# Soft-capped attention followed by soft mixture-of-experts on one core: other parts and packets for the second-layer weights, other places for the weight loads, and shorter dispatch sums

## The chip, the cores and the metric

The kernel runs on 1 core of one Trainium2 chip, as one launch. The time is device microseconds (us) of that core. Before the change three runs gave 284.57 us in the median (280.42, 284.57 and 288.0). The core has five engines with their own instruction streams: TensorE (PE: matmuls, weight loads, transposes), VectorE (DVE), ScalarE (ACT), GpSimd (POOL) and SyncE (SP). DMA transfers run on 16 DMA engines, and reach them here by two queues: SP's (q1, plain copies) and POOL's (q0, which also casts float32 to bfloat16 on the way; called the casting queue below).

## The reference

Attention with 8 batches, 12 heads, 448 tokens and 64 dimensions a head, float32:

```python
scores = q @ k.T / 8;  scores = 30 * tanh(scores / 30)
attn = softmax(scores);  x = attn @ v            # -> x: 3584 tokens x 768
```

Then a soft mixture of experts with 8 experts of 4 slots each (32 slots), w1 of 8 x 768 x 1024 and w2 of 8 x 1024 x 768:

```python
logits = x @ phi                                  # 3584 x 32
d = softmax(logits, over all 3584 tokens)         # dispatch
slot_in = d.T @ x                                 # 32 x 768
slot_out[e] = relu(slot_in[e] @ w1[e]) @ w2[e]    # 4 slots for each expert
c = softmax(logits, over the 32 slots)            # combine
out = c @ slot_out                                # 3584 x 768
```

No output can be written before the dispatch sums over all tokens are complete, both layers of the experts have run, and so all of w1 and w2 have been read.

## The kernel before

**Attention.** Work goes by quads of four heads (24 quads, Q) and by pairs of heads (48 pairs). A quad's q and k come in by casting DMAs (`load`, two 224-KB loads a quad, started when the transposes of the quad two earlier have freed the buffer), are turned by PE (`K`, `J`) and copied by DVE (`k`, `j`). Scores of three 128 x 448 chunks lie in one PSUM tile (`Q`, L432); ACT takes tanh from it (`T`, L442); six chunks form a group, whose exp is done either by ACT (`E`, L446) or by eight DVE steps that build it as a polynomial (`p`, L466 to L474). PE multiplies by v (`A`, `B`, `t`, `u`, L495), DVE normalises (`r`, `m`), PE turns x (`X`, `y`), and a batch's logits (`L`), their exp (`e`), dispatch sums (`S`, added up by `s`) and transposed exps (`R`, `c`) follow.

**The order** is written out by hand as a string of jobs, `PROGRAM`, for all engines at once; every engine runs its part of it in that order. Three kinds of job are only fillers for PE: `N` (a 128x512 matmul into a spare tile), `F` (57 columns) and `G` (64 columns).

**Weights.** `M` jobs start a casting DMA of weights each, on POOL, in the order of `wjobs`: 16 halves of w1 (768 KB each in bfloat16), which stay in SBUF; then the parts of w2 that SBUF has no room for, which are cast into DRAM tiles (`w2d`, "spilled" or parked); then three kept parts of w2 (`w2u`) that go to SBUF. There are 64 blocks of w2, each of 128 rows; a part is four blocks. A part holds the same 128 rows of four experts, so a packet of it is one row of 768 elements (1536 bytes written). 6 parts are parked whole; 7 are parked as two halves of 384 columns (768 bytes a packet).

**Reload.** When attention tiles come free, SP copies the parked parts back to SBUF (`reload`, L162): 20 loads, 6 of 768 KB and 14 of 384 KB. One (job `O0`) goes out in `PROGRAM`, the others behind it, each waiting for the tiles whose place it takes. The order of SP's queue is: v loads, these 20, then the output.

**The end.** Layer 1 (L859), relu, transposes of the hidden values (`h_transp`, L876), then layer 2 (`layer2`, L887) in two sweeps over the 16 parts: first the left 384 columns of all (half 0), then the right 384 (half 1). The accumulated half goes to SBUF as `so[0]` (L935) and `so[1]` (L943). Eight left half-tiles of output are computed between the parts of the second sweep (`EARLY`, L916 to L920) and stored at once (L904); the rest of the 28 token tiles follow, DVE and ACT in turn, with the stores on SP.

**Dispatch sums.** `slot_sums` gives, for a batch, the 193 columns of slot inputs and of the sum of exps z; `z_mms` (L599) makes z with 16 matmuls of one column, four for each group of tokens so that it stands in all four groups of 32 partitions. `slot_add` (L664) adds them up in `slz`, and `zacc`, its last column, is inverted into `rz` at the end.

Of the kernel before, what the change touches and what calls it, by code (L numbers as in the profile page):

```python
# [9 lines left out]
F32 = mybir.dt.float32  # L10
BF16 = mybir.dt.bfloat16
# [27 lines left out]
def kernel(  # L39
# [31 lines left out]
    WHOLE = 6  # L71
# [28 lines left out]
    slz = consts.tile([P, NJ * NS + 1], F32, name="slacc")  # L100
    slacc = slz[:, 0:NJ * NS].rearrange("p (j s) -> p j s", s=NS)
    zacc = slz[:, NJ * NS:]
# [12 lines left out]
    blocks = [(i, ft, gg) for i in range(E // 4) for ft in range(NFT) for gg in range(4)]  # L115

    def w2_src(n0, n):

        i, ft, gg = blocks[n0]
        return bass.AP(tensor=moe_w2.tensor,  # L120
                       offset=((4 * i + gg) * F + ft * P) * D,
                       ap=[[D, P], [F * D, n], [1, D]])
# [8 lines left out]
    def load_part(dst, n0, half=None):  # L131
        src = w2_src(n0, 4)
        if half is not None:
            src = bass.AP(tensor=src.tensor, offset=src.offset + half * HD,
                          ap=[[D, P], [F * D, 4], [1, HD]])
        pool.dma_start(out=dst, in_=src)
# [3 lines left out]
    late = len(w2_parts) - KEPT + NFREE  # L140
    w2_kept = w2_parts[:NFREE] + w2_parts[late:]
    w2_spilled = [(n0, None) for n0 in w2_parts[NFREE:NFREE + WHOLE]]
    w2_spilled += [(n0, half) for half in range(2) for n0 in w2_parts[NFREE + WHOLE:late]]

    dram = ctx.enter_context(tc.tile_pool(name="dram", bufs=1, space=bass.MemoryType.DRAM))
    w2d = {(n0, half): dram.tile([P, 4, D if half is None else HD], BF16, name=f"w2d{n0}_{half}")
           for n0, half in w2_spilled}
    wjobs += [(load_part, w2d[part], *part) for part in w2_spilled]
# [12 lines left out]
    def reload(n, t):  # L161
        sp.dma_start(out=t, in_=w2d[w2_spilled[n]])  # L162
        w2t[w2_spilled[n]] = t

    def reload_raw(n):
        t = rawt[:, 2 - 2 * n:4 - 2 * n, :].rearrange("p n s -> p (n s)")
        reload(WHOLE + n, t[:, 0:4 * HD].rearrange("p (n d) -> p n d", d=HD))

# [29 lines left out]
p0.4 M0 T5 Q6 k2 p0.5 N1.0 T6.1 Q7 N3.0 V1.0 j2 V1.1 T7 Q8 p0.6 T8.6 Q9 N3.0 p3.0 T9 Q10 M1 p3.1  # L198
N1.0 T10.3 Q11 p0.7 J3.0 E2 p3.2 A0.1 t0 j3 B0 u0 p3.3 K3.0 Q12 T11 G14.12 k3 G6.12 p3.4 T12.4 Q13
r0 p3.5 A1.0 M2 T13 Q14 t1 B1 m0 T14.2 F8 u1 Q15 r1 m1 T15 p3.6 N1.0 X0.0 y0 J4.1 E4 x0 p7.0 A2.0  # L200
Q16 p3.7 t2 M3 F9 E5 j4 B2 u2 p7.1 K4.1 k4 Q17 p7.2 T16.7 A3.1 r2 p7.3 B3 t3 u3 T17 Q18 G6.18 m2
T18.0 r3 p7.4 N1.0 A4.0 Q19 M4 m3 E6 F12 p7.5 J5.1 t4 F4 B4 j5 T19 p7.6 Q20 K5.1 T20.5 Q21 k5 u4 r4
A5.1 T21 p7.7 t5 B5 m4 M5 E8 u5 p10.0 X1.0 Q22 r5 p10.1 y1 Q23 x1 G19.23 T22.6 p10.2 N1.0 K6.0 m5
T23 Q24 p10.3 X2.1 T24.3 y2 Q25 x2 M6 k6 T25 Q26 p10.4 J6.0 T26.1 L0.1 j6 p10.5 Q27 e0 E11 S0.1
p12.0 A6.0 p10.6 B6 Q28 E9 t6 u6 G23.28 r6 s0 M7 m6 R0.1 p12.1 A7.0 T27 c0 B7 p12.2 t7 u7 K7.1 T28.2
r7 k7 m7 E13 p12.3 A8.0 J7.1 Q29 p10.7 Q30 F9 M8 p12.4 T29 B8 G13.30 j7 T30.4 p12.5 Q31 t8 J8.1 T31
u8 Q32 r8 p12.6 T32.7 Q33 G6.33 m8 T33 Q34 p15.0 K8.0 j8 M9 T34.0 p15.1 N1.1 A9.1 t9 E14 p12.7 B9
p15.2 u9 Q35 k8 N1.0 Q36 p15.3 T35 A10.0 t10 B10 T36.5 r9 p15.4 u10 Q37 m9 M10 T37 Q38 p15.5 J9.1
T38.6 Q39 j9 G6.39 r10 T39 p15.6 A11.1 t11 B11 E16 u11 Q40 r11 m10 G10.40 m11 K9.0 p18.0 A12.1 t12
# [623 lines left out]
    for n in (0, WHOLE + 2, WHOLE + 3, 1, 2, 3, WHOLE + 1, *range(4, WHOLE), *range(WHOLE + 4, len(w2_spilled))):  # L833
        if n == WHOLE + 1:
            reload_raw(1)
            continue
# [7 lines left out]
    def w2_half(n, half):  # L844
        n0 = n - n % 4
        if (n0, half) in w2t:
            return w2t[n0, half][:, n % 4, :]
# [164 lines left out]
```

## Time and profile before

| | |
|---|---|
| median of 3 runs | 284.57 us (280.42 to 288.0) |
| the profiled execution's own time | 281.34 us |
| its span, first to last instruction | 279.4 us |
| granted TensorE clock, mean | 0.968 |
| ACT busy | 245.1 us, 88% |
| DVE busy | 242.2 us, 87% |
| PE busy | 236.1 us, 85% |
| casting queue (q0) | 31840 packets, 35.77 MB, 75.1% of 16 DMA engines' span |
| SP's queue (q1) | 22880 packets, 32.95 MB, 35.8% |

The attention fills the time to about 235 us; experts and output fill the rest. The share of a queue is the time that its packets took over 16 engines' time; packets of the two queues may be under way in one engine together, so the sum can pass 100%. A group's row gives line, engine, operation, tiles and count, then busy time and the mean of one in ns, then the idle time of the engine ahead of it and who ended it. In the page's rows by slices of the span one slice is a fortieth.

### The profile page before, as it was taken

The numbers are of one execution on the slowest core, as the hardware profiler recorded it, in microseconds if no ns is written. First come the engines' busy times: TensorE is split into PE (matmuls) and PEld (weight loads), VectorE is DVE, ScalarE is ACT, GpSimd is POOL, SyncE is SP. The second block draws the span as 40 slices with busy tenths as digits, with TensorE's granted clock in tenths as the row PEclk, the third lists the DMA queues.
The fourth block names the chain that finished last, engine by engine and source line by source line (L and its number), as shares of the span: only waits on it lengthen the run. The fifth ranks groups of instructions, "written<-read, shape, count | busy, mean of one in ns | idle before, by whom it ended". The sixth has DMA issues, their size and how long they took to land.

```text
span 279.4 us, 9803 instructions
## 1 busy us (share of the span) xinstructions
PE 236.1 (85%) x4151; PEld 150.8 (54%) x4151; DVE 242.2 (87%) x361; ACT 245.1 (88%) x192; POOL 157.6 (56%) x253
## 2 busy tenths in 40 slices
PE   8899889987998988988888898988898998997710
PEld 6435555653565656565665665656566686543300
DVE  3799999998999999999999999999999995337740
ACT  4999999998899999999999999999999997246620
POOL 8489777365586578466885678989725420200000
PEclk9999999997799999999999999999999999999975
DMA  6999999999999999999999999999999999979996
GB/s 181 214 170 220 223 222 223 225 216 223 218 225 229 225 211 227 228 227 218 219 227 228 208 221 219 218 213 216 227 223 245 286 296 405 406 284 378 422 424 268
DMA packets 55051, 69.56 MB, mean 249 GB/s; under 512 B 5984, under 2 KB 45024, under 8 KB 55008
## 3 DMA queue, kind: packets, MB, share of 16 engines
q0 software_dynamic: 31840, 35.77, 75.1%
q1 hardware_dynamic: 22880, 32.95, 35.8%
q8 instruction: 32, 0.52, 0.7%
q10 hardware_dynamic: 288, 0.23, 0.3%
q14 instruction: 11, 0.09, 0.1%
HBM read 93.68 MB, written 21.23 MB: 411 GB/s over the span
## 4 chain that ended last, share of the span: by engine, by line
ACT 44%; DVE 21%; PE 16%; DMA 9%; issue 3%; POOL 2%; DVEq 0%; POOLq 0%; ACTq 0%
ACT ex L442 21%; ACT ex L446 11%; DMA raws<-in_q_dram 6%; ACT exg L442 6%; ACT exg L446 4%; PE pv L495 4%; DVE xq L507 3%; PE sc L432 3%; PE so_ps L887 2%; DMA out_dram<-ob 2%; DVE ex L473 2%; PE hp L859 2%; DVE xf L468 2%; DVE xp L470 2%; DVE xp L472 2%
## 5 line engine op out<-in xcount | busy, mean ns | idle before, releaser
L442 ACT ACTIVATE ex<-sc 128x1344 f16<-128x1344 f32 (+1 forms) x87 | 108.8, 1365 | 2.2 <-PE sc L432 2.1
L432 PE MATMUL sc<-qT,kT 64*128 64x448 bf16 x384 | 68.1, 357 | 8.5 <-ACT ex L442 5.2
L446 ACT ACTIVATE ex<-ex 128x2688 bf16<-128x2688 f16 x27 | 68.4, 2553 | 0.0
L495 PE MATMUL pv<-vbd,ex 128*128 128x65 bf16 (+2 forms) x1041 | 55.5, 201 | 5.4 <-DVE xT L564 1.9
L407 POOL CAST vbd<-vraw 128x384 bf16<-128x384 f32 x46 | 34.1, 742 | 42.4 <-DMA vraw<-in_v_dram 16.5
L495 PEld LDWEIGHTS <-ex 128*128 128x128 bf16 (+1 forms) x1070 | 42.9, 101 | 20.5 <-issue 5.7
L411 POOL CAST vbd<-vraw 64x64 bf16<-64x64 f32 x92 | 48.0, 521 | 2.8
L442 ACT ACTIVATE exg<-sc 128x1344 f16<-128x1344 f32 x26 | 33.2, 1344 | 1.0 <-PE sc L432 1.0
L432 PEld LDWEIGHTS <-kT 64*128 64x128 bf16 x384 | 19.1, 94 | 24.5 <-issue 11.1
L507 DVE TENSOR_TENSOR xq<-pv,rec 128x448 bf16<-128x448 f32 x47 | 28.5, 613 | 0.4
L446 ACT ACTIVATE exg<-exg 128x2688 bf16<-128x2688 f16 x11 | 27.6, 2510 | 0.0
L389 PEld LDWEIGHTS <-raws 128*64 128x64 bf16 x616 | 19.9, 111 | 12.4 <-issue 10.4
L472 DVE TENSOR_TENSOR xp<-xp,xf 128x2688 f16<-128x2688 f16 x17 | 26.4, 1555 | 0.0
L470 DVE TENSOR_TENSOR xp<-xp,xf 128x2688 f16<-128x2688 f16 x17 | 26.2, 1544 | 0.0
L278 POOL DMA_DIRECT2D raws<-in_q_dram x22 | 18.2, 827 | 13.7 <-PE qps L389 8.4
L473 DVE TENSOR_TENSOR ex<-ex,xp 128x2688 uint16<-128x2688 uint16 x15 | 23.1, 1541 | 0.0
L495 PE MATMUL pv<-vbd,exg 128*128 128x65 bf16 (+2 forms) x322 | 20.9, 201 | 2.5 <-DVE xq L507 1.3
L278 POOL DMA_DIRECT2D raws<-in_k_dram x22 | 16.9, 770 | 8.6 <-PE kps L389 8.5
L495 PEld LDWEIGHTS <-exg 128*128 128x128 bf16 (+1 forms) x322 | 14.6, 102 | 8.1 <-issue 4.1
L389 PE MATMUL kps<-ident,raws 128*64 128x128 bf16 x308 | 13.1, 225 | 3.0 <-DVE qT L401 0.9
L471 DVE TENSOR_SCALAR xp<-xp 128x2688 f16<-128x2688 f16 x17 | 15.6, 918 | 0.0
L469 DVE TENSOR_SCALAR xp<-xf 128x2688 f16<-128x2688 uint16 x17 | 14.9, 874 | 0.0
(134 smaller groups left out, 379.0 us busy)
## 6 DMA issues: line engine op xcount, KB each, us to landing
w1b<-in_moe_w_dram POOLq DMA_DIRECT2D x16, 768.0 KB, 12.7
out_dram<-ob SPq DMA_DIRECT2D x8, 768.0 KB, 7.5
vraw<-in_v_dram SPq DMA_DIRECT2D x92, 64.0 KB, 5.7
w2d<-in_moe_w_dram POOLq DMA_DIRECT2D x14, 384.0 KB, 12.0
raws<-in_q_dram POOLq DMA_DIRECT2D x22, 224.0 KB, 10.5
raws<-in_k_dram POOLq DMA_DIRECT2D x22, 224.0 KB, 11.1
w2d_None<-in_moe_w_dram POOLq DMA_DIRECT2D x6, 768.0 KB, 14.5
w2t<-w2d_None SPq DMA_DIRECT2D x6, 768.0 KB, 9.1
```

The lines of the kernel that those rows point to most:

```text
L278: pool.dma_start(out=t, in_=quad_ap(nm, Q))
L389: pe.transpose(dst, src[:, h, c * DH:(c + 1) * DH], ident)
L407: pool.tensor_copy(part(t[:, h, :, :], 0, [(CS + 2) * W, 2], [W, CS], [1, DH]), part(raw, 0, [(CS + 1) * DH, 2], [DH, CS], [1, DH]))
L411: pool.tensor_copy(t[r, h, CS + n, 0:DH], raw[r, CS * DH:(CS + 1) * DH])
L432: pe.matmul(sc[:, u, 0:S], qkT["k", Q][r, at:at + P], qkT["q", Q][r, :, n * HP:n * HP + HP], start=(c > 0 or n == 0), stop=(c > 0 or n == 1))
L442: act.activation(exs[j][:, half * CS + u0:half * CS + u1, :].bitcast(F16), sc[:, u0:u1, 0:S], ACT.Tanh, scale=qk_scale / cap)
L446: act.activation(exs[j][:, u0:u1, :], exs[j][:, u0:u1, :].bitcast(F16), ACT.Exp, scale=cap)
L470: lambda: dve.tensor_tensor(p, p, f, op=ALU.mult),
L472: lambda: dve.tensor_tensor(p, p, f, op=ALU.mult),
L473: lambda: dve.tensor_tensor(y, y, p, op=ALU.add),
L495: pe.matmul(out_, exs[j][:, u, q0:q0 + (HP if tail else P)], v_, start=(c == 0 and g == gs[0] < NF), stop=(c >= NT - 2), skip_group_check= ...
L507: dve.tensor_tensor(xq[Q][:, h, s0:s1, :], pv[:, 0:s1 - s0, 0:DH], recs.pop(pr).to_broadcast([P, s1 - s0, DH]), op=ALU.mult)
```

## The change

- **Parts and packets of w2.** A block is still 128 rows of one expert, but a part is now four blocks (512 rows) of the same expert, two parts to an expert. Within a pair of blocks the rows are dealt in turn (even rows to one, odd to the other), so a partition reads two rows that stand side by side and a packet holds 3072 bytes. `h_transp` takes the hidden values in the same order, by every second element.
- **Kept and parked.** Parts 0 to 2 are kept, parts 3 to 15 are parked whole, in 13 casting DMAs instead of 20. Each weight matmul still takes 4 blocks side by side; the four column groups now hold four blocks of the same expert and sum up in the last product.
- **Reload.** 16 loads in place of 20: parts 3 and 4 in two loads of two blocks each (384 KB), parts 5 to 14 whole (768 KB), part 15 as two column halves (384 KB, 768 bytes a packet). Left and right halves of a part otherwise come together.
- **Places of `M`.** 32 jobs instead of 39, set at other places in `PROGRAM`; 5 of the `N` jobs and two `F4` are gone, one `G23` is `G25`, one `G12` is `G11`; all other jobs stand in the same order.
- **Dispatch sums.** z of a batch by 4 matmuls of 32 columns instead of 16 of one; `slot_add` adds 224 columns instead of 193; two DVE operations pick the sum out by the identity once, at the end.

```diff
-    WHOLE = 6
+    WHOLE = 10
...
-    blocks = [(i, ft, gg) for i in range(E // 4) for ft in range(NFT) for gg in range(4)]
+    blocks = [(e, ft) for e in range(E) for ft in range(NFT)]
...
-                       offset=((4 * i + gg) * F + ft * P) * D,
-                       ap=[[D, P], [F * D, n], [1, D]])
+        return bass.AP(tensor=moe_w2.tensor, offset=(e * F + ft * P) * D,
+                       ap=[[2 * D, P], [2 * P * D, 2], [1, 2 * D]])
...
+    w2_kept = w2_parts[:KEPT]
+    split = len(w2_parts) - WHOLE - 1
+    w2_spilled = w2_parts[KEPT:]
...
+    reload_tl(split)
+    reload_tl(split - 2, 2, 4)
+    reload_tl(split - 1, 0, 2)
+    for n in range(split + 1, split + 4):
+        reload_tl(n)
+    reload_raw(1)
+    for n in range(split + 4, split + WHOLE):
+        reload_tl(n)
+    for half in range(2):
+        reload_tl(split + WHOLE, 0, 4, half, half + 1)
...
-        z_mms(b, ps[:, SW:SW + 1], True, True)
-        slot_mms(b, ps[:, 0:SW].rearrange("p (j s) -> p j s", s=NS), range(NG), range(NJ))
+        slot_mms(b, sums, range(NF), range(NJ))
+        for g in range(NF):
+            pe.matmul(twice(ps[:, SW:SW + NS], SW + NS), ones, twice(es[b][:, g, :], 0), start=False, stop=False,
+                      skip_group_check=True)
+        pe.matmul(ps[:, SW:SW + NS], ones[0:HP, :], es[b][0:HP, NF, :], start=False, stop=True,
+                  skip_group_check=True)
+        slot_mms(b, sums, (NF,), range(NJ))
...
+    dve.tensor_tensor(zps, ident.rearrange("p (a s) -> p a s", s=NS),
+                      bass.AP(tensor=zsum.tensor, offset=zsum.offset, ap=[zsum.ap[0], [0, 4], [1, NS]]),
+                      op=ALU.mult)
+    dve.reduce_sum(zacc, zps.rearrange("p a s -> p (a s)"), axis=mybir.AxisListType.X)
...
-            pe.matmul(src[:, ft - t0, :, :], hbs[i][:, ft * P:(ft + 1) * P], own,
+            pe.matmul(src[:, ft - t0, :, :], hbs[i].rearrange("p (q f r) -> p q f r", r=2, f=P)[:, ft // 2, :, ft % 2], own,
```

The first lines of `PROGRAM` before and after (a letter is a kind of job, the numbers its arguments):

```diff
-p0.4 M0 T5 Q6 k2 p0.5 N1.0 T6.1 Q7 N3.0 V1.0 j2 V1.1 T7 Q8 p0.6 T8.6 Q9 N3.0 p3.0 T9 Q10 M1 p3.1
+p0.4 T5 Q6 k2 p0.5 N1.0 T6.1 Q7 N3.0 V1.0 j2 V1.1 T7 Q8 M0 p0.6 T8.6 Q9 N3.0 p3.0 T9 Q10 p3.1 N1.0
...
-A5.1 T21 p7.7 t5 B5 m4 M5 E8 u5 p10.0 X1.0 Q22 r5 p10.1 y1 Q23 x1 G19.23 T22.6 p10.2 N1.0 K6.0 m5
-T23 Q24 p10.3 X2.1 T24.3 y2 Q25 x2 M6 k6 T25 Q26 p10.4 J6.0 T26.1 L0.1 j6 p10.5 Q27 e0 E11 S0.1
+m4 E8 u5 p10.0 X1.0 Q22 M4 r5 p10.1 y1 Q23 x1 G19.23 T22.6 p10.2 K6.0 m5 T23 Q24 p10.3 X2.1 T24.3 y2
+Q25 x2 k6 T25 Q26 p10.4 J6.0 T26.1 L0.1 j6 p10.5 Q27 e0 E11 S0.1 M5 p12.0 A6.0 p10.6 B6 Q28 M6 E9 t6
```

More of the change, by code (lines that the diff above doesn't have):

```diff
@@ L885, in layer2 @@
         for n in range(n0, n0 + 4):
-            i, ft, gg = blocks[n]
-            pe.matmul(so_ps[half][32 * gg:32 * gg + NS, :],
-                      hpad[:, 4 * i + gg, ft, :],
+            e, ft = blocks[n]
+            pe.matmul(so_ps[half][32 * (n - n0):32 * (n - n0) + NS, :],
+                      hpad[:, e, ft, :],
                       w2_half(n, half),
```

148 lines of the change are left out of this document (70 added, 78 removed).

## The prediction

> **What bounds the kernel now.** First the page: how busy each engine and each queue is, and when.
>
> ```profile
> PE 236.1 (85%) x4151; PEld 150.8 (54%) x4151; DVE 242.2 (87%) x361; ACT 245.1 (88%) x192; POOL 157.6 (56%) x253
> ACT  4999999998899999999999999999999997246620
> DMA  6999999999999999999999999999999999979996
> q0 software_dynamic: 31840, 35.77, 75.1%
> L442 ACT ACTIVATE ex<-sc 128x1344 f16<-128x1344 f32 (+1 forms) x87 | 108.8, 1365 | 2.2 <-PE sc L432 2.1
> L442 ACT ACTIVATE exg<-sc 128x1344 f16<-128x1344 f32 x26 | 33.2, 1344 | 1.0 <-PE sc L432 1.0
> ```
>
> ACT is full from the second slice to the 34th (about 235 us), the DMA engines from the second to the last but one. Over the whole attention ACT idles 2.2 + 1.0 = 3.2 us ahead of its tanh. The change leaves ACT's work as it is, so 3.2 us is all that attention can give.
>
> Where that idle time lies is told by ACT's one dip, slices 9 and 10, read with the chain of waits in order of time and with stretches of 3.41 us around it (columns: PE, weight loads, DVE, ACT, POOL busy; granted clock; DMA share; GB/s).
>
> ```profile
> 52.59 13.55 DMA raws<-in_q_dram
> 66.19 0.58 PE qps L389 x14
> 67.51 1.30 ACT exg L442
> 63.63:67.04 3.41, 1.93 (x35) 1.19 (x33) 2.22 (x5) 2.91 (x3) 0.30 (x1) 1.00 1.14 229
> 67.04:70.45 3.41, 2.84 (x24) 1.11 (x22) 3.41 (x6) 2.76 (x3) 2.71 (x4) 0.50 1.20 213
> 70.45:73.86 3.41, 3.35 (x44) 2.33 (x40) 3.41 (x5) 3.33 (x2) 1.62 (x2) 0.50 1.15 218
> 73.86:77.28 3.42, 3.42 (x44) 1.64 (x41) 3.42 (x5) 2.79 (x3) 2.89 (x4) 1.00 1.20 217
> ```
>
> A q load issued at 52.59 took 13.55 us in a full casting queue; the transposes that it feeds began the moment it came. PE had worked 1.93 of 3.41 us, and its clock then stood at 0.50 for 6.8 us. ACT lost 0.50 + 0.65 + 0.08 + 0.63 = 1.86 us in the four stretches.
>
> The end is a relay of transfers: reload, then output.
>
> ```profile
> 236.00:240.00 4.00, 3.91 (x93) 2.39 (x96) 0.91 (x5) 0.45 (x2) 1.81 (x1) 1.00 1.01 416
> 244.00:248.00 4.00, 4.00 (x89) 2.21 (x85) 0.32 (x2) 0.85 (x2) 0.00 (x0) 1.00 0.92 369
> 248.00:252.00 4.00, 4.00 (x57) 1.36 (x56) 2.60 (x5) 2.33 (x4) 0.00 (x0) 1.00 0.63 231
> 260.00:270.00 10.00, 4.79 (x31) 2.23 (x29) 6.87 (x8) 5.29 (x6) 0.00 (x0) 0.92 1.02 424
> GB/s 241 301 282 284 364 284 292 225 264 283 280 242 282 249 358 391 232 307 355 362 427 399 445 410 399 420 410 427 393 423 431 374 410 403 420 420 338 220 58 215
> 232.10 2.63 ACT L753 ACTIVATE ex<-ex 128x1536 bf16<-128x1536 f16 x3
> 247.06 0.48 ACT L935 CAST so<-so_ps 128x384 bf16<-128x384 f32 x1 [2.69 <-PE so_ps L887]
> 248.61 9.37 SPq L904 DMA_DIRECT2D out_dram<-obh  x13
> ```
>
> The GB/s row covers 214 to 250 us in slices of 0.9 us: reload runs at some 410 until 246.4 and has drained by about 248.6 (338, 220, 58). Half 0 was complete at 247.06, the first store went out at 248.61, and later the stores fill the engines (1.02, 424 GB/s). So the end moves by as much as half 0 moves: what is late there, the output is late by.
>
> **Part 1: packets.** Two stretches of the DMA view give the price of a cast packet: one in which w1 (2048 bytes) is cast beside q and k, one in which w2's halves are. The rows under them are issues of the whole run.
>
> ```profile
> q0 software_dynamic: 7520, 10.64, 98.6%
> q0 software_dynamic: 7361, 5.68, 104.5%
> w2d<-in_moe_w_dram POOLq DMA_DIRECT2D x14, 384.0 KB, 12.0
> w2d_None<-in_moe_w_dram POOLq DMA_DIRECT2D x6, 768.0 KB, 14.5
> w2u<-in_moe_w_dram POOLq DMA_DIRECT2D x3, 768.0 KB, 15.5
> ```
>
> In 50 to 110 us, 0.986 x 16 x 60 us / 7520 = 125.9 ns for 1415 bytes; in 165 to 200, 1.045 x 16 x 35 / 7361 = 79.5 ns for 772 bytes. That is 0.072 ns a byte and 24 ns a packet. w2 before: 14 x 512 packets of 768 bytes (79 ns) and 9 x 512 of 1536 (135 ns), 1188 us over 16 engines, 74 us. After: 16 x 256 packets of 3072 bytes, 245 ns by that line (never seen here; bounds: 79 ns if only the packet counted, 316 ns at 79.5 / 772 a byte): 63 us. I take 245 ns: the queue has 11 us less to do in some 215.
>
> The Trainium skill, DMA: Bandwidth & Descriptors, section Specifications, asks for at least 512 bytes a transfer for line rate. By that 768-byte packets are fast already and nothing is saved; the two rows disagree (9.7 bytes a ns against 11.2), but do not reach 3072.
>
> The 11 us are not on the path by themselves: ACT was waiting in one place only. What counts is that q load (`J6`). Before, M5 and M6 (4.1 us of queue each: 384 packets of 2048 bytes at 172 ns over 16) stood between `K5` and it; after, M4 alone, M5 coming behind it. It lands over 4 us sooner, where 1 us would do. I walked the other q and k loads through the queue in `PROGRAM`'s order with these prices: the worst is later by some 2.6 us and had over 10 us to spare. **Term: -1.8 us** (0 if another load takes over the stall, -3.2 if all ACT idling goes).
>
> **Part 2: fewer fillers, shorter sums.** Five `N` and two `F4` go, so PE idles more. The barest place:
>
> ```profile
> 30.20 0.39 PE L670 MATMUL junk<-ones 128*128 128x512 bf16 x1 [0.48 <-DVE xq L507]
> 28.80:32.20 3.40, 2.50 (x43) 1.39 (x39) 3.08 (x6) 3.40 (x4) 2.33 (x4) 1.00 1.18 220
> 225.11 0.24 PE L599 MATMUL slps<-ones,E 128*32 128x1 bf16 x12
> 225.20 0.17 PE L599 MATMUL slps<-half,E 128*32 128x1 bf16 x4
> 226.53 0.31 DVE L664 TENSOR_TENSOR slacc<-slps,slacc 128x193 f32<-128x193 f32 x1
> 234.22 0.18 DVE L503 RECIPROCAL rec<-pvl 128x4 f32<-128x4 f32 x1 [1.28 <-PE pvl L495]
> ```
>
> 2.50 - 0.39 = 2.11 of 3.40 us, 62% busy, against 57% (1.93 of 3.41) where the clock fell. I cost it at nothing, and keep the fall as a rival. z falls from 16 matmuls (0.26 us) to 4, a tenth of a us of PE a batch that ACT, full there, doesn't see; `slot_add` grows by 31 of 193 columns, 0.05 us. The two new DVE operations fall into the 1.28 us that DVE idles before 234.22; about 0.3 us if that cover went. **Term: 0.**
>
> **Part 3: half 0 needs all parts.** SP's queue in 50 to 110 us and in 250 to 279, and layer 2's matmuls:
>
> ```profile
> q1 hardware_dynamic: 3518, 2.52, 17.1%
> q1 hardware_dynamic: 4074, 10.82, 93.4%
> L887 PE MATMUL so_ps<-w2t,hpad x96: 324/326/337, 244.1 to 251.3; 128*32 128x384 bf16 x96
> ```
>
> Before, 20 loads carried 6 x 768 + 14 x 384 = 9984 KB, and the last seven (2688 KB) were right halves that half 0 doesn't read. At 0.41 MB a us half 0's data was in 6.7 us before the end, about 242; PE, busy throughout, set the pace up to 247.06. After, as many KB come, but all except the last 384 KB are ahead of half 0's end. The size of its pieces has a price too. 50 to 110 us gives 46.7 ns for 716 bytes; 250 to 279 gives 106 ns for 2656; so 48 ns for 768 bytes and 119 for 3072. Part 15's halves take 512 x 48 / 16 = 1.55 us each instead of 128 x 119 / 16 = 0.95. The end of reload goes from 248.6 to 249.8, half 0's last data comes 1.55 before it, 248.25; four matmuls side by side (0.33) and a little for the semaphore make 248.8 where 247.06 stood. **Term: +1.8 us** (0 if reload runs far enough ahead that PE still sets the pace; +4 if the last cast part, 256 x 245 / 16 = 3.9 us of queue, falls wholly into the reload). Behind it wait `so[0]`, the early tiles, and every store on SP.
>
> **Part 4: the last jobs.**
>
> ```profile
> 228.00:232.00 4.00, 3.67 (x89) 3.07 (x85) 3.30 (x9) 4.00 (x3) 0.00 (x0) 1.00 0.95 323
> q1 hardware_dynamic: 1241, 3.41, 62.5%
> q0 software_dynamic: 761, 1.12, 39.9%
> ```
>
> The two queue rows are of 214 to 230 us, where both share the engines. The last kept part's job stands where it stood, so its transfer begins near 217 as before. Behind the last q load four parts of 3.9 us wait (M27 to M30) where 2.5 + 4.3 + 4.3 us waited (512 packets each, of 79, 135 and 135 ns). That queue drains perhaps 1.6 us later and takes engine time from the first reloads. Since 228 to 232 ran at 323 GB/s, below the later 416, most of it can be made up.
>
> **Term: +0.3 us** (-1 to +1.6).
>
> **Sum.** -1.8 + 0 + 1.8 + 0.3 = +0.3 us against 281.34, the profiled execution's own time (span 279.4 and 1.9 around it). That execution lies 3.2 below the median of the three runs, 284.57. The middle of the four times (280.42, 281.34, 284.57, 288.0) is 283.0, and I lay the sum on it: **283.3 us**. A measurement of a kernel that spreads so can tell about 2% from no change, 278.9 to 290.3 around the median.
>
> **Rivals.** *Reload keeps ahead (0.20).* For it: with 11 us less casting, the queue may leave room for the first loads; 323 GB/s shows slack. Against: the loads wait for attention's tiles, which come free when they did, and the last cast job isn't sooner. Then term 3 and 4 fall away and attention may give all 3.2: 283.0 - 1.8 = 281.2 down to 279.8, and under 278.9 with a calm run.
>
> *Reload comes later (0.17), the slower side.* One mechanism: casts still under way after 214 take the engines' time from the reload, with 245-ns packets in place of 135. It decides from the point where half 0's data is later than 247, and costs 1 us a us: up to +4 at term 3 and +1.6 at term 4. 283.0 - 1.8 + 4 + 1.6 = 286.8, slower than before. For it: casts held 39.9% of the engines in 214 to 230; against: its last job was as large before.
>
> *The clock falls (0.08).* 62% at 30 us, or any stretch that the missing fillers thin out. A fall cost 1.86 us here; two, with the stall gone, give 283.3 + 3.7 = 287.0, and later stalls more. The Trainium skill, TensorE: Matmul & The Clock Gate, Part 1, says that the gate watches windows of about 3.4 us that run free of the kernel; the fall after one thin stretch of 3.41 us and its two-stretch length agree, and by it the same thin place would fall in some runs only.
>
> *Packets are no cheaper (0.05).* The change doesn't do what it says: at 316 ns, a part takes 5.1 us; M27 to M31 then end 5 x 1.1 = 5.6 us later, inside the reload: 283.0 - 1.8 + 1.8 + 5.6 = 288.6.
>
> **Chances.** Forecast 0.50, and the four rivals as given. Range 278.5 to 288.5: from the quick reload in a calm run to the dearest rival; about two in ten lie outside. Faster by over 2% only where reload keeps ahead and no stall is left, about half of that rival and a little of the forecast: 0.12. Slower by over 2% needs two mishaps or a restless run: 0.08. Within: 0.80.
>
> **What would show it.** Right: no clock fall near 67 us and ACT's idling ahead of L442 near 1.4 us; q0 near 24160 packets (31840 - 11776 + 4096) and 71% of the span; PE waiting for a reload within half 0's sweep; `so[0]` copied some 17 us after the last exp (L753) begins, where 247.06 - 232.10 = 15.0 stood. Wrong: `so[0]` no later (term 3), the clock down in new places (term 2), a share of q0 as before (term 1). What I may have missed is contention that no single row prices: v loads on SP, and PE's transposes, now beside longer packets.

## The result: slower, and the profile after

The changed kernel took 290.9 us in the median of six runs (290.15 to 293.76) where the kernel before, run beside it, took 283.75 (280.42 to 288.0). The ratio is 1.032, with a 95% interval of 1.024 to 1.040. The forecast, 283.3 us, and the whole of its range (to 288.5) lie below that. The profiled execution took 291.03 us, its span is 288.8, against 281.34 and 279.4. Runs of one kernel spread by some 2% (those of the kernel before lie in two heaps, near 280 and near 284 us), the ratios leave the slowest out, and one experiment, `no_wait_late`, was profiled in such a slow run, so that only its times are read.

The page of after, the lines that answer to those of before (busy time, slices, clock, GB/s by slices, the casting queue, and ACT's two groups of tanh):

```profile
PE 236.1 (82%) x4055; PEld 149.5 (52%) x4055; DVE 243.0 (84%) x363; ACT 245.2 (85%) x192; POOL 152.6 (53%) x246
ACT  4999999999999999999999999999999942037610
PEclk9999999998999999999999999999999999869975
GB/s 175 215 181 123 222 224 221 224 221 219 192 235 224 216 214 231 228 220 230 228 185 217 220 231 162 215 226 228 226 226 225 330 420 416 328 123 358 407 410 234
q0 software_dynamic: 24048, 35.77, 69.6%
L438 ACT ACTIVATE ex<-sc 128x1344 f16<-128x1344 f32 (+1 forms) x87 | 107.6, 1337 | 1.9 <-PE sc L428 1.9
L438 ACT ACTIVATE exg<-sc 128x1344 f16<-128x1344 f32 x26 | 33.2, 1342 | 0.2 <-PE sc L707 0.2
```

The engines are busy as long as they were; ACT's dip in slices 9 and 10 is gone. New are the hole behind slice 33, where ACT shows 0 and the transfers fall to 123 GB/s, and a lower clock there. Also new is a thin fourth slice (123 GB/s). Rows of the timeline, in order of time, tell the end: last exp, the last parts of half 0, `so[0]`, first store, `so[1]`.

```profile
231.06 2.63 ACT L755 ACTIVATE ex<-ex 128x1536 bf16<-128x1536 f16 x3
...
245.74 0.35 PE L902 MATMUL so_ps<-w2t,hpad 128*32 128x384 bf16 x4 [0.37 <-DMA w2t<-w2d]
247.60 0.35 PE L902 MATMUL so_ps<-w2t,hpad 128*32 128x384 bf16 x4 [1.51 <-DMA w2t<-w2d]
249.49 0.35 PE L902 MATMUL so_ps<-w2t,hpad 128*32 128x384 bf16 x4 [1.54 <-DMA w2t<-w2d]
251.46 0.51 PE L902 MATMUL so_ps<-w2t,hpad 128*32 128x384 bf16 x4 [1.62 <-DMA w2t<-w2d]
252.41 0.51 PE L902 MATMUL so_ps<-w2t,hpad 128*32 128x384 bf16 x4 [0.43 <-DMA w2t<-w2d]
252.96 0.48 ACT L950 CAST so<-so_ps 128x384 bf16<-128x384 f32 x1 [9.27 <-PE so_ps L902]
255.31 11.08 SPq L919 DMA_DIRECT2D out_dram<-obh  x13
259.72 0.56 DVE L958 CAST so<-so_ps 128x384 bf16<-128x384 f32 x1 [0.65 <-PE so_ps L902]
```

and of before, the row that the prediction didn't need:

```profile
251.84 0.56 DVE L943 CAST so<-so_ps 128x384 bf16<-128x384 f32 x1 [0.65 <-PE so_ps L887]
```

PE now waits for five reloads in a row within half 0. With the rows of before this makes a sum for the whole difference of the spans. Attention ends 1.0 us sooner (232.10 to 231.06). From the last exp to `so[0]` it is 21.9 us instead of 15.0: +6.9. From `so[0]` to `so[1]` 6.8 instead of 4.8: +2.0. From `so[1]` to the end of the span 29.1 instead of 27.6: +1.5. Together +9.4, which is 288.8 - 279.4. These are single executions; the medians of all runs differ by 7.2 us.

Why `so[1]` lags is in the stretches around (PE, weight loads, DVE, ACT, POOL; clock; DMA share; GB/s), of after:

```profile
243.68:247.09 3.41, 2.03 (x44) 1.14 (x44) 0.29 (x1) 0.01 (x1) 0.00 (x0) 1.00 1.03 419
247.09:250.50 3.41, 0.69 (x8) 0.20 (x8) 0.00 (x0) 0.00 (x0) 0.00 (x0) 1.00 1.01 380
250.50:253.91 3.41, 2.01 (x24) 0.80 (x23) 0.00 (x0) 0.48 (x1) 0.00 (x0) 0.50 0.37 121
253.91:257.33 3.42, 3.42 (x25) 0.66 (x22) 1.24 (x2) 1.17 (x2) 0.00 (x0) 0.50 0.34 120
```

PE was busy 0.69 of 3.41 us, and then its clock stood at 0.50 for 6.8 us, just when `so[0]` was done and the second sweep was to run.

Why the reload is late is in the queues. Of before, in this order: q0 and q1 in 20 to 30 us; q0 from 0 to 120; q0 in 150 to 200; q1 and q0 in 216 to 224; q1 from 0 to 232 (packets, MB, share):

```profile
q0 software_dynamic: 943, 1.64, 91.1%
q1 hardware_dynamic: 709, 0.52, 19.3%
...
q0 software_dynamic: 14756, 19.06, 90.9%
...
q0 software_dynamic: 10242, 8.33, 105.4%
...
q1 hardware_dynamic: 524, 1.54, 53.3%
q0 software_dynamic: 469, 0.71, 51.4%
...
q1 hardware_dynamic: 16691, 15.49, 24.4%
```

The same of after:

```profile
q0 software_dynamic: 558, 0.91, 59.0%
q1 hardware_dynamic: 645, 0.47, 19.3%
...
q0 software_dynamic: 14326, 18.15, 88.2%
...
q0 software_dynamic: 4761, 8.22, 89.9%
...
q0 software_dynamic: 501, 1.44, 91.1%
q1 hardware_dynamic: 502, 0.34, 18.3%
...
q1 hardware_dynamic: 16417, 13.98, 22.1%
```

Three things are to be seen. The casting queue lost 0.73 MB between 20 and 30 us, where `M0` now comes late; at 120 us it is 0.91 MB behind. In 150 to 200 us it moved about as many bytes as before (8.22 against 8.33 MB) at a share of 89.9% in place of 105.4%: larger packets lowered the share and hardly the time. (Each kernel has a thin stretch of casting in there, near 170 us. In 180 to 200 us, where neither has, it was 3.41 MB at 109.1% before and 3.57 MB at 95.4% after, 5% more bytes.) And in 216 to 224 us, when before had SP's reload under way, casts still held the engines, and SP got one packet for each of theirs (502 to 501), 0.34 MB in place of 1.54. By 232 us SP's queue is 1.51 MB behind; at the reload's 0.41 MB a us that is 3.7 us. Since the reloads wait for attention's tiles, the last exp is the better mark to count to: by then SP's queue had moved 15.54 MB before and 13.58 MB after, 1.96 MB or 4.8 us less.

### The profile page after: what moved, and what is told of

It reads as the page before. It is cut to its first block, busy times and chain, and to the rows that moved or that the text cites. A ratio compares the mean times of both kernels' runs of the same rounds, so it can differ in the third digit from the quotient of the medians.

```text
span 288.8 us, 9602 instructions
## 1 busy us (share of the span) xinstructions
PE 236.1 (82%) x4055; PEld 149.5 (52%) x4055; DVE 243.0 (84%) x363; ACT 245.2 (85%) x192; POOL 152.6 (53%) x246
## 3 DMA queue, kind: packets, MB, share of 16 engines
q0 software_dynamic: 24048, 35.77, 69.6%
## 4 chain that ended last, share of the span: by engine, by line
ACT 40%; DVE 28%; PE 12%; DMA 12%; issue 2%; DVEq 0%; SPq 0%; ACTq 0%
ACT ex L438 18%; ACT ex L442 10%; DMA w2t<-w2d 8%; ACT exg L438 7%; ACT exg L442 4%; DVE ex L469 4%; DVE xq L503 4%; DVE xp L466 3%; DVE xp L468 3%; PE sc L428 2%; PE pv L491 2%; DMA out_dram<-ob 2%; DVE xp L467 2%; DVE ex L470 2%; DVE kT L394 2%
## 5 line engine op out<-in xcount | busy, mean ns | idle before, releaser
L438 ACT ACTIVATE ex<-sc 128x1344 f16<-128x1344 f32 (+1 forms) x87 | 107.6, 1337 | 1.9 <-PE sc L428 1.9
L403 POOL CAST vbd<-vraw 128x384 bf16<-128x384 f32 x46 | 38.6, 840 | 55.3 <-DMA vraw<-in_v_dram 17.7
L442 ACT ACTIVATE ex<-ex 128x2688 bf16<-128x2688 f16 x27 | 67.6, 2516 | 0.0
L491 PEld LDWEIGHTS <-ex 128*128 128x128 bf16 (+1 forms) x1070 | 43.0, 101 | 22.9 <-issue 5.3
L407 POOL CAST vbd<-vraw 64x64 bf16<-64x64 f32 x92 | 49.3, 536 | 2.8
L274 POOL DMA_DIRECT2D raws<-in_q_dram x22 | 16.6, 755 | 11.5 <-PE qps L385 9.1
L933 DVE TENSOR_SCALAR obh<-op,winv 128x384 f32<-128x384 f32 x10 | 6.0, 615 | 13.0 <-PE op L931 13.0
```

Of the source, the lines that this page charges most:

```text
L274: pool.dma_start(out=t, in_=quad_ap(nm, Q))
L403: pool.tensor_copy(part(t[:, h, :, :], 0, [(CS + 2) * W, 2], [W, CS], [1, DH]), part(raw, 0, [(CS + 1) * DH, 2], [DH, CS], [1, DH]))
L407: pool.tensor_copy(t[r, h, CS + n, 0:DH], raw[r, CS * DH:(CS + 1) * DH])
L438: act.activation(exs[j][:, half * CS + u0:half * CS + u1, :].bitcast(F16), sc[:, u0:u1, 0:S], ACT.Tanh, scale=qk_scale / cap)
L442: act.activation(exs[j][:, u0:u1, :], exs[j][:, u0:u1, :].bitcast(F16), ACT.Exp, scale=cap)
L491: pe.matmul(out_, exs[j][:, u, q0:q0 + (HP if tail else P)], v_, start=(c == 0 and g == gs[0] < NF), stop=(c >= NT - 2), skip_group_check= ...
```

## The experiments

Ratios are to the kernel before in runs beside, with a 95% interval. Its medians in the six batches were 282.35, 283.27, 283.29, 280.35, 280.38 and 284.42 us. The batches ran on different chips, so kernels are also compared by the marks in their own traces, one execution each.

### Less casting, or only the sums: where the loss isn't

`no_kept`: the three kept parts' casts are cut to 64 columns of one block, and layer 2 takes the weights of part 5 for them.

```diff
-        load_part(w2u[n], w2_kept[n])
+        pool.dma_start(out=w2u[n][:, 0, 0:64], in_=bass.AP(tensor=moe_w2.tensor, offset=n * 512 * D, ap=[[D, P], [1, 64]]))
...
-        return w2u[n // 4][:, n % 4, half * HD:(half + 1) * HD]
+        return w2_half(w2_parts[split] + n % 4, half)
```

> The changed kernel without the casts of the three kept parts (only 64 columns of one block of each are loaded, and layer 2 uses part 5's weights in their place, so part of w2 is left out). Everything else as changed. Theory A: some 13 us of casting less behind the last q load; the casting queue is empty by about 213, v loads and the reload have the engines from then, half 0 is complete before 249 us in the profile, and the time is 282 to 285. Theory B: half 0 still waits for all of the reload, which is as long as before: 288 or more.

Measured: 282.82 us, ratio 1.004 (0.999 to 1.008); `so[0]` 15.5 us behind the last exp. With 2.3 MB of the 35.77 not cast the loss is gone: it hangs on how long the casting lasts. (The kernel before was not run with the same cut.)

`sums_only`: the kernel before with the new dispatch sums (`slot_sums`, `slz`, `zsum`, the two DVE operations) and nothing else.

```diff
-    slz = consts.tile([P, NJ * NS + 1], F32, name="slacc")
+    slz = consts.tile([P, NJ * NS + NS], F32, name="slacc")
...
-        z_mms(b, ps[:, SW:SW + 1], True, True)
+        for g in range(NF):
+            pe.matmul(twice(ps[:, SW:SW + NS], SW + NS), ones, twice(es[b][:, g, :], 0), start=False, stop=False,
+                      skip_group_check=True)
...
```

> The kernel before with the new dispatch sums alone (z by 4 matmuls, 224 columns added, the two operations at the end). All theories: no difference that can be measured, 282 to 285.5; z matmuls of a batch take about 0.1 us instead of 0.26. Over 286 would mean that the sums carry part of the loss.

Measured: 283.08 us, 1.004 (0.999 to 1.009): no change that the times can tell. Its trace does show a longer end, which comes up again under "Behind so[1]".

### Places of the weight jobs

`old_places`: the changed kernel with its 32 jobs where the kernel before has theirs. `mended_places`: the same, with `M6` behind `J6`. `m0_early`: only `M0` to `M2` moved back. `before_j6` and `before_gap`: the kernel before, with `M6` behind `J6`, and with `M0` to `M2` as late as in the changed kernel.

```diff
 old_places, mended_places, m0_early
-p0.4 T5 Q6 k2 p0.5 N1.0 T6.1 Q7 N3.0 V1.0 j2 V1.1 T7 Q8 M0 p0.6 ...
+p0.4 M0 T5 Q6 k2 p0.5 N1.0 T6.1 Q7 N3.0 V1.0 j2 V1.1 T7 Q8 p0.6 ...
 before_gap: the reverse of it, in the kernel before
 before_j6, mended_places
-Q25 x2 M6 k6 T25 Q26 p10.4 J6.0 T26.1
+Q25 x2 k6 T25 Q26 p10.4 J6.0 M6 T26.1
```

> The changed kernel with its weight jobs put back at the places of before (a whole parked part at the place of the part or the pair of halves that it replaces); parts, packets, sums and fillers as changed. Theory A (the reload is late because the casting queue was left idle early and still had 11 us of casts to do at 214 us, where 6.3 were left before): the idle gap of the queue near 21 us goes, its last cast ends 3 to 5 us sooner, and the time falls from 290.9 to 285 to 287. Theory B (half 0 is late only because both halves of a part are reloaded together): 290 to 291, whatever the queue does. Theory C (thinner PE work and its clock): 290 to 291.

> The changed kernel with its weight jobs at the places of before (as in the run old_places), except that M6 comes behind the transposes J6, so that the q load ahead of them isn't late. Theory A: no idle gap of the queue near 21 us and no stall near 67 us; attention ends as in the changed kernel (last exp at about 231 us), casts end 3 to 5 us sooner than there, half 0 is complete at about 249: 285 to 287. If the stall near 67 us comes back in another place: 288 to 290.

> The changed kernel with only M0, M1 and M2 moved to where the kernel before has them. Theory that the end of casting and reload together is what counts, so that every idle us of the casting queue comes back at the end: the gap of 3.4 us at 21 us goes, so[0] comes 2 to 3.4 us sooner and the time is 287 to 288.5 us. Rival, that a gap so early is made up by slower jobs later (waits move, they do not go): so[0] within 1 us of the changed kernel's 253, 290 to 291 us.

> The kernel before with one job moved: M6 behind the transposes J6 (its 768-KB cast starts behind the q load that was late near 66 us). Term 1 of the prediction: stall and clock fall near 67 us go, ACT idles some 1.5 us less, and the time falls by 1 to 1.8 us against the kernel before. Rival: the queue is as full, the wait only moves to another load: within 0.5 us of before.

> The kernel before with M0, M1 and M2 put in as late as the changed kernel has them: its casting queue then idles about 3 us near 21 us. Theory that the slack of the kernel before (its last seven reloads, 2688 KB, are not needed by half 0) hides such a lateness: so[0] within 0.5 us of 246 to 247, 282.5 to 284 us. Rival, that lost casting time costs the kernel before as much as the changed one: 285.5 to 287 us.

The last column is what SP's queue had moved by the last exp.

| | time, ratio (interval) | cast by 30, 120 us | last exp | exp to `so[0]` | SP by last exp |
|---|---|---|---|---|---|
| before | | 3.36, 19.06 MB | 232.10 | 15.0 | 15.54 MB |
| after | 290.9, 1.032 (1.024 to 1.040) | 2.68, 18.15 | 231.06 | 21.9 | 13.58 |
| old_places | 289.18, 1.024 (1.016 to 1.033) | 3.07, 18.82 | 233.80 | 18.2 | 15.58 |
| mended_places | 290.25, 1.032 (1.024 to 1.040) | 3.33, 19.05 | 235.35 | 17.0 | 15.56 |
| m0_early | 291.74, 1.032 (1.024 to 1.040) | 3.33, 18.12 | 231.23 | 22.3 | 13.62 |
| before_j6 | 283.12, 1.003 (0.998 to 1.009) | 3.36, 19.06 | 234.30 | 14.8 | 15.59 |
| before_gap | 284.73, 1.009 (1.003 to 1.014) | 2.68, 18.51 | 235.15 | 14.8 | 15.50 |

Rows of `old_places` (last exp, `so[0]`), then of `mended_places`:

```profile
233.80 2.63 ACT L755 ACTIVATE ex<-ex 128x1536 bf16<-128x1536 f16 x3
252.03 0.48 ACT L950 CAST so<-so_ps 128x384 bf16<-128x384 f32 x1 [5.41 <-PE so_ps L902]
```

```profile
235.35 2.63 ACT L755 ACTIVATE ex<-ex 128x1536 bf16<-128x1536 f16 x3
252.32 0.48 ACT L950 CAST so<-so_ps 128x384 bf16<-128x384 f32 x1 [4.23 <-PE so_ps L902]
```

What follows: with the old places the casting keeps its lead, SP's queue is as far by the last exp as before, and the stretch behind that exp shrinks by 3.7 to 4.9 us. But a load comes late again (of q near 67 us in `old_places`, of k near 174 us in `mended_places`) and attention ends 2.7 to 4.3 us later than in the changed kernel, which eats it: `so[0]` comes only 0.6 to 0.9 us sooner. The later attention holds the transfers too: in 216 to 224 us the engines moved 159 GB/s in `mended_places`, where the changed kernel moved 226. Lead and attention are traded for each other, and neither run came down to the 285 to 287 us that the theory of the lead gave. The early gap alone isn't the cause: `m0_early` has its 3.33 MB by 30 us and by 120 is where the changed kernel is, since the later jobs stand at places that let the queue run thin (in 48 to 54 us it cast 0.57 MB, the changed kernel 0.99); the theory that every idle us comes back at the end fell. `before_gap`: in the kernel before, the same late start leaves 14.8 us behind the exp. That doesn't show that its slack hides a late reload, since by that exp SP's queue had caught up (15.50 MB); what it lost (1.4 us) it lost in attention, where ACT idled 5.6 us ahead of its tanh instead of 3.2. `before_j6` takes away the wait on which term 1 rests, and ACT idled 5.1 us elsewhere: the wait moves.

### Packets

`rows_1536`: the changed kernel, w2 in packets of 1536 bytes.

```diff
-                       ap=[[2 * D, P], [2 * P * D, 2], [1, 2 * D]])
+                       ap=[[D, P], [P * D, 4], [1, D]])
```

> The changed kernel with w2 dealt in rows as before, so that the casts of w2 go in 1536-byte packets (512 a part) in place of 3072; parts, order, places, reload and sums as changed. My price of the prediction: 16 parts x (4.3 - 3.9) = 6 us more of queue, all of it behind 120 us, reload and end later by as much: 294 to 297. Theory D with packets in turn: the queue's bytes flow as fast, and v loads and the first reloads get some 80 GB/s beside it instead of 45, so the end is the same or sooner: 287 to 291.

Measured: 290.88 us, 1.035 (1.028 to 1.042). In 216 to 224 us SP and the casting queue here (q1, q0):

```profile
q1 hardware_dynamic: 499, 1.63, 55.6%
q0 software_dynamic: 524, 0.78, 53.5%
```

SP has its 1.63 MB, but the casts go on past 236 us, and `so[0]` comes 22.9 us behind the exp. What one queue gains the other loses, so the size of the packets by itself isn't what made the reload late. The prediction's price had given 294 to 297 us.

`cast_price` computes nothing of the function: it only casts w2 in packets of 768, 1536 and 3072 bytes and w1 in packets of 2048, four stretches alone and four beside a stream of v loads on SP.

```diff
+    for kind in (768, 1536, 2048, 3072):
+        for r in range(R):
+            cast(kind, m, f"a{kind}_{r}")
+            m += 1
...
+    for n in range(160):
+        w = 256 if n % 2 else 192
+        dst = gate[0:HP, 0:w] if n == 0 else tiles[n % 8][:, 0:w]
+        sp.dma_start(out=dst, in_=bass.AP(tensor=v.tensor, offset=(n % 90) * S * DH, ap=[[S, HP], [1, w]]))
```

> Casting alone: no attention, no experts, only five parts' worth of casts (768 KB each) of 768-, 1536-, 2048- and 3072-byte packets one after the other, first with nothing beside them, then beside a stream of v-like loads (768 and 1024 bytes a packet) on SP that never lets up; then a part of the output is filled with zeros (everything else is left out). My price of the prediction (24 ns a packet and 0.072 ns a byte): alone 155, 182, 190 and 200 GB/s. Theory D (casts are paid by bytes once the queue is full, so larger packets save little): about 165 to 180 GB/s for all. For the stream beside them: if the engines take packets of the two queues in turn, it gets about one packet of 900 bytes for each cast packet, some 110, 80, 65 and 48 GB/s; if they share by time or bytes, about the same beside all four.

Alone, 768 bytes (4.2 to 22.8 us) and 3072 bytes (61.2 to 78.5):

```profile
q0 software_dynamic: 4956, 3.70, 130.2%
...
q0 software_dynamic: 1266, 3.69, 108.2%
```

Beside SP's stream, the four sizes in order (85.0 to 104.0, 106.1 to 129.7, 131.2 to 153.3, 154.7 to 175.0):

```profile
q0 software_dynamic: 3607, 2.68, 90.6%
q1 hardware_dynamic: 2334, 1.68, 36.3%
...
q0 software_dynamic: 2464, 3.69, 85.4%
q1 hardware_dynamic: 2461, 1.76, 30.8%
...
q0 software_dynamic: 1871, 3.70, 88.1%
q1 hardware_dynamic: 1870, 1.34, 25.0%
...
q0 software_dynamic: 1259, 3.67, 91.1%
q1 hardware_dynamic: 1256, 0.91, 18.2%
```

A 3072-byte packet took 1.082 x 16 x 17.3 / 1266 = 237 ns (245 was estimated). But alone, 3.7 MB took 18.6 us in small packets and 17.3 in large ones, 199 and 213 GB/s: 7%, where the sum of packet times, by 1.302 x 18.6 against 1.082 x 17.3, fell by 23%. Small packets overlap. Both expected prices for casting alone (155 to 200 and 165 to 180 GB/s) were too low; that the size matters little is as theory D had it. A cast reads float32, twice the bytes counted here, so 213 GB/s written are some 427 read. Beside SP's stream both queues together move 229, 231, 228 and 226 GB/s, whatever the size; casting gets 141, 156, 167 and 181 of it, SP 88, 75, 61 and 45. From 1536 bytes up the engines take the queues in turn, one packet each (2464 to 2461, 1259 to 1256), so a larger cast packet is paid by SP. The Trainium skill, DMA: Bandwidth & Descriptors, section "Queues, rings and completion order", says that an engine goes round the queue rows with work, a packet at a time; these rows and the 501 to 502 of after agree. The 3607 to 2334 at 768 bytes don't speak against it: SP's stream moved 88 GB/s there and 89 with no casts beside it (2.32 MB in 178 to 204 us), so it had no more packets to give.

### What half 0 waits for, and the clock

`both_halves`: the right halves of parts 0 to 13 run beside the left ones in the first sweep. `spin`: PE is kept busy in the waits. `no_wait_late`: layer 2 takes the weights of parts 5 to 8 for parts 12 to 15; the transfers stay.

```diff
 both_halves
         layer2(n0, 0)
+        if n0 < n2 - 8:
+            layer2(n0, 1)
 spin
+        if n0 >= 40:
+            busy(18, spin)
         layer2(n0, 0)
 no_wait_late
     def w2_half(n, half):
+        if n >= 48:
+            n -= 28
```

> The changed kernel with layer 2 taking the right half of parts 0 to 13 right behind the left half, so that only the right halves of the last two parts follow so[0]; so[1] is then ready under 2 us after so[0], where 6.8 us lay between; the ten left half-tiles follow. Theory A and B: so[0] still at about 253 us in the profile, so[1] at about 255, and of the 8 us by which so[1] was late some 4 to 5 come back: 286 to 287. If only the first store counts (output bound by DMA from there): 289 to 291.

> The changed kernel with PE kept busy in the waits of layer 2's first half: from n0 = 40 on, six matmuls on constants stand ahead of each part. In the changed kernel PE is busy 20% of 247 to 250.5 us and its clock then stands at 0.50 until 257.3; so[1] follows so[0] by 6.8 us, against 4.8 before. Theory that the clock adds to the loss: no fall near 250, so[0] as late as in the changed kernel (253), so[1] about 2 us sooner (257.5), 289 to 290 us. Rival, that the output transfers alone decide from the first store on: clock full, so[1] sooner, time unchanged at 290 to 291 us.

> The changed kernel with every transfer as it is, but layer 2 takes the weights of parts 5 to 8 in place of those of parts 12 to 15, so that half 0 needs nothing of the last four reloads (the function differs in that). Theory that half 0's need of the whole reload makes the loss: PE isn't held, so[0] at 246 to 248, no clock fall near 250, and since the stores still stand behind a reload that ends near 253 in the same queue, 284.5 to 287 us. Rival, that the reload's own lateness makes all of it by keeping the engines from the output: 289 to 291 us with so[0] sooner. Were only PE's wait to count, and the late reload nothing, 282 to 283.

`both_halves`: 290.22 us, 1.031 (1.024 to 1.037). `so[1]` came 4.7 us sooner (255.01), the first store only 0.6 (254.76), and the time stayed within the noise: an early `so[1]` buys little here, as the rival of the first store had it. `spin`: 288.95 us, 1.022 (1.012 to 1.031); the stretches of `spin`:

```profile
247.09:250.50 3.41, 3.41 (x28) 1.43 (x26) 0.00 (x0) 0.00 (x0) 0.00 (x0) 1.00 1.00 351
250.50:253.91 3.41, 3.41 (x37) 1.56 (x37) 0.00 (x0) 0.48 (x1) 0.00 (x0) 1.00 0.16 50
253.91:257.33 3.42, 3.42 (x48) 1.06 (x50) 2.44 (x4) 2.10 (x4) 0.00 (x0) 1.00 0.48 173
```

The clock stays at 1.00, `so[0]` comes at 253.23 as late as ever, and `so[1]` 4.8 us behind it: the 2.0 us were the clock's, as that theory had it. `no_wait_late`: 283.71 us, 1.009 (1.004 to 1.014). I had expected 284.5 to 287; that the reload itself is late costs less than I thought, and PE's waits for its last four parts (in either half) make most of the loss.

### The function whole, half 0 relieved

`halves_last`: the last seven parts reloaded by halves, left ones first, so that 2688 KB again come behind half 0's need. `halves_old_places`: with the old places as well. In both a half is read out of whole rows, in pieces of 768 bytes, where a whole part goes in packets of some 5 KB. `halves_apart` and `halves_apart_old` cast these seven parts as two halves into tiles of their own (and the other parts in 1536-byte packets), so that they come back in 3072-byte pieces.

```diff
-    for n in range(split + 4, split + WHOLE):
-        reload_tl(n)
     for half in range(2):
-        reload_tl(split + WHOLE, 0, 4, half, half + 1)
+        for n in range(split + 4, split + WHOLE + 1):
+            reload_tl(n, 0, 4, half, half + 1)
 halves_apart, halves_apart_old: also
+    w2d[n0] = [dram.tile([P, 4, HD], BF16, name=f"w2d{n0}_{half}") for half in range(2)]
```

> The changed kernel with its last seven parts reloaded by halves, all left halves first: the last 2688 KB are again not needed by half 0, as in the kernel before. Casts, places and bytes stay. Theory that half 0's need of the whole reload makes the loss: half 0's data is in 2304 KB sooner, 5.5 us at 0.42 MB a us, so[0] comes at 247 to 248.5 though the reload still ends near 253, the clock stays up, 283.5 to 286 us. Rival, that the late reload itself holds the output: 288 to 291 us.

> As halves_last, with the weight jobs at the places of the kernel before, which gives the casting its old lead (in old_places 18.8 MB were cast by 120 us, in the changed kernel 18.2, before 19.1). Theory that need and lead are the whole loss: so[0] some 15 us after the last exp, as before; the exp itself comes 1 to 2 us later than before by its stall near 70 us, so 283 to 285 us. Rival, that the larger packets cost by themselves in the tail: the interval stays at 17 to 18 us, 286 to 289 us.

> The changed kernel with its last seven parts cast as two halves into tiles of their own (packets of 768 bytes in casting, as before) and reloaded left halves first in pieces of 3072 bytes; the other parts cast in packets of 1536 bytes. Theory that half 0's need and then the idle or slow stretch behind it make the larger share of the loss: so[0] near 248.5, the reload at 410 GB/s ends near 253, so[1] by 254, ratio to before 1.007 to 1.015 (what is left is the later start of the reload). Rival, that the late reload alone makes it: 1.022 or more, as in halves_last.

> As halves_apart, with the weight jobs at the places of the kernel before. Theory that need and lead are the whole loss: ratio to before 0.997 to 1.007, so[0] 15 us behind the last exp and so[1] 4.8 behind it. Rival, that something else in the change costs: 1.012 or more.

| | time, ratio (interval) | last exp | to `so[0]` | `so[1]` | span |
|---|---|---|---|---|---|
| halves_last | 288.88, 1.029 (1.025 to 1.034) | 230.71 | 18.1 | 257.15 | 286.9 |
| halves_old_places | 287.63, 1.025 (1.018 to 1.033) | 234.74 | 15.1 | 256.19 | 285.4 |
| halves_apart | 286.88, 1.022 (1.012 to 1.032) | 230.78 | 17.8 | 255.65 | 284.9 |
| halves_apart_old | 289.12, 1.029 (1.019 to 1.039) | 235.54 | 15.3 | 256.13 | 285.3 |

`so[0]` came about as the theory had it: at 248.78 and 248.58 with half 0 relieved, and 15.1 and 15.3 us behind the exp with the casting lead as well. `so[1]` and the times didn't; all four times lie where the rivals had them. In `halves_last` the reload itself got slower; SP's queue in 236 to 246 us, of after and then of `halves_last`:

```profile
q1 hardware_dynamic: 829, 4.13, 100.5%
```

```profile
q1 hardware_dynamic: 3826, 3.41, 106.3%
```

413 against 341 GB/s, so `so[1]` waited. Stored apart, the halves were worth about 1% against the changed kernel (1.022 against 1.032, with intervals that overlap), some 3 us. What is left in the span of `halves_apart`, +5.5 us, is +2.8 behind the exp (17.8 instead of 15.0), +2.3 from `so[0]` to `so[1]` and +1.7 behind it, with 1.3 less in attention; in `halves_apart_old` it is an attention that ends 3.4 us later than before and +1.6 behind `so[1]`. No version of the change beat the kernel before.

### Behind so[1]

From `so[1]` to the end the same work took 29.0 to 29.8 us in most kernels with the new sums, and 27.6 to 27.9 in the others. The sums widen `slacc` by 31 columns and add a tile, which in the built program moves every large buffer from a multiple of 4096 bytes to 128 bytes past it. `before_shift` makes that move alone, `after_trim` takes it back, with `winv`, `rz`, `zacc`, `ones32` and `half1` in one tile.

```diff
 before_shift, in the kernel before
+    pad = consts.tile([P, 32], F32, name="pad")
+    dve.memset(pad[:, 0:1], 0.0)
 after_trim, in the changed kernel
+    small = consts.tile([P, 32], F32, name="small")
...
-    zacc = consts.tile([P, 1], F32, name="zacc")
+    zacc = small[:, 29:30]
```

> The kernel before with an unused tile of 128 bytes a partition ahead of the large buffers, so that they begin 128 bytes past the multiples of 4096 at which they stand in the kernel before, as in the changed kernel. Theory that the place in SBUF slows the transfers: stores of 216 ns in place of 207, so[1] to the end 29 us or more in place of 27.6, 1.2 to 1.8 us more than the kernel before (ratio 1.004 to 1.007). Rival, that the new operations or tiles of the sums do it: no change, 27.6 us and a ratio within 0.002 of 1.

> The changed kernel with winv, rz, zacc, ones32 and half1 in one tile, which saves 128 bytes a partition and puts the large buffers back at multiples of 4096. Theory that the place in SBUF slows the transfers: stores of 207 ns again, so[1] to the end 27.6 to 28 us in place of 29.1, the time 289 to 289.8 us against 290.9. Rival: 29 us and 290.5 to 291.5 us as in the changed kernel.

SP's queue in four us of stores of 1536 bytes (4 to 8 us behind `so[1]`) of before, `before_shift`, after and `after_trim`:

```profile
q1 hardware_dynamic: 1113, 1.59, 106.6%
```

```profile
q1 hardware_dynamic: 1021, 1.47, 101.9%
```

```profile
q1 hardware_dynamic: 1024, 1.47, 101.8%
```

```profile
q1 hardware_dynamic: 1113, 1.59, 106.5%
```

The place in SBUF alone switches a store packet between 61 ns (1.066 x 64 us / 1113) and 64. The time didn't follow. `before_shift` ran 281.34 us, ratio 0.991 (0.986 to 0.996): under 2%, and lower where both expectations had it the same or higher; why stays open. Its `so[1]` to the end is 27.8 us although its packets take 64 ns. `after_trim`: 290.2 us (288.07 to 290.95), its last stretch 28.3 us instead of 29.1, its ratio 1.023 (1.016 to 1.031), which overlaps the changed kernel's. The effect on the packets is shown, one on the time is not. The 29.3 us of `sums_only` point to the new sums for the longer end; which of their operations or tiles makes it stays open.

## Why the prediction was wrong, point by point

Set against the two profiled executions, term 1 stood at -1.8 and came to -1.0; terms 3 and 4 stood at +2.1 together and came to +6.9, from the last exp to `so[0]`; the clock behind that wait (+2.0) and the last stretch (+1.5) had no term. The step that failed is that the reload was taken to run as early as before: by the last exp SP's queue had moved 13.58 MB where 15.54 stood, and half 0, which now needs nearly all of it, waited.

**Part 1, packets: its step failed.** The packet came out as estimated (237 against 245 ns), and the wait for the q load at 67 us went: ACT idles 1.9 + 0.2 us ahead of its tanh where 2.2 + 1.0 stood, and the last exp comes 1.0 us sooner (foretold 1.8; PE's clock still fell near 70 us, the 8 in its row, and ACT waited 0.66 us at 73.2). That it went is not shown to be the doing of the new order ahead of `J6`: in `before_j6` the same relief only moved the waiting elsewhere, so there is luck in it. What failed is "the queue has 11 us less to do". It summed packet times, and the two rows it rested on had shares of 98.6% and 104.5% beside another queue: packets overlap, and the limit here is bytes a us. The share fell to 69.6% of a longer span, and the bytes didn't come sooner. The sum doesn't use the 11 us directly; term 4 does by its prices for the queue's last jobs, which come from the same two rows. The places of `M`, which the part priced only at `J6`, made them later by 0.91 MB at 120 us. The Trainium skill's rule of 512 bytes (DMA: Bandwidth & Descriptors, Specifications), weighed there, would have said that nothing is saved, and with 7% in `cast_price` it came nearer than my row.

**Part 2, fillers and sums: right as far as the times tell.** No fall of the clock near 30 us, and `sums_only` shows no cost that its times can tell. What it overlooked is the end: behind `so[1]` most kernels with the new sums take 1 to 2 us longer in their traces (+1.5 in the changed kernel), and the cause of that stays open.

**Part 3, half 0 needs all parts: right in kind, mis-sized.** PE does wait within half 0. With the reload as far by the last exp as before (`old_places`, `mended_places`), this alone made 17.0 to 18.2 us out of 15.0, so +2.0 to +3.2 where +1.8 stood. The term took the reload to run as early as before. It began late: the casting queue, 0.91 MB behind since 120 us, had 1.84 MB left at 216 us where 0.92 stood, filled the engines until about 227 us and gave SP one packet for one. With half 0 relieved, the lateness costs +2.8 to +3.1 (`halves_apart` 17.8, `halves_last` 18.1); both together +6.9, by the rows of after. Before, the last 2688 KB, 6.7 us of reload, were slack for half 0; that they would have hidden all of this lateness no run shows.

**Part 4, the last jobs: too small.** +0.3 stood for what became 1.51 MB, 3.7 us of reload, at 232 us, and 1.96 MB by the last exp. The rival "reload comes later" named the mechanism with the casts that take the reload's time; its price (+5.6 with term 3) stopped short because it let the casting queue keep its lead and left the clock out.

**The clock.** The rival looked for thin stretches in attention. The fall came where term 3's wait itself empties PE, and cost 2.0 us between `so[0]` and `so[1]` (`spin`). A wait in which PE works 0.69 of 3.41 us should have had that price added.

## What to carry to other kernels

Price a queue by the bytes that it moves a us beside its neighbours, never by the sum of its packets' times; a share over 100% says that packets overlap. Where two queues share the engines, look who gets which share of packets: larger packets on one took from the other here, but smaller ones only turned that round, and what is late on either shows far behind, at the next stage. Before taking a slack out (here 2688 KB that the first sweep didn't need), list what lateness it may hide now, and add the clock's price to a wait in which TensorE stands for most of a stretch as long as those above.

## What the runs showed that was not expected

- Casting beside a plain stream moves 226 to 231 GB/s in all, for cast packets of 768 to 3072 bytes; the plain reload alone moved 413.
- The engines alternate between the two queues one packet for one (1259 to 1256, 501 to 502).
- Reading 768-byte pieces out of 1536-byte rows ran at 341 GB/s, whole parts, in packets of some 5 KB, at 413.
- Buffers 128 bytes past a multiple of 4096 make a 1536-byte store packet 64 ns instead of 61. The Trainium skill, DMA: Bandwidth & Descriptors, section "How a descriptor splits into AXI transactions", says that a transfer that doesn't start at a multiple of 256 bytes fetches from the boundary below it, which would lengthen it; the rows agree in direction.
